# Block-sparse attention and a cosine MLP: one transfer that transposes P for two units, and query halves copied by VectorE

## The chip, the cores and the metric

The kernel runs on one core of a Trainium2 chip. The metric is the device time of one execution in microseconds. Work is spread over TensorE (PE, matrix products), VectorE (DVE), ScalarE (ACT), GpSimd (POOL) and SyncE (SP). SP computes nothing here: it issues every transfer of the kernel, in order, on one queue (SPq in the rows), and 16 DMA engines move the data.

## What is computed

Four batches, 8 heads, 768 positions, 64 columns per head, blocks of 32 positions (24 blocks). Attention is masked by blocks, and its output, 3072 x 512, goes through a feed-forward part of width 2048:

```python
scores = scale * np.matmul(q, k.transpose(0, 1, 3, 2))
mask = np.abs(blk_i - blk_j) <= 1
mask = mask | (blk_i == 0) | (blk_j == 0) | (blk_i == n_blocks - 1) | (blk_j == n_blocks - 1)
for qb in range(n_blocks):
    for kb in sampled_blocks[qb]:
        mask[qb*block:(qb+1)*block, kb*block:(kb+1)*block] = True
scores = np.where(mask, scores, -1000000000.0)
attn = np.exp(scores - np.max(scores, axis=-1, keepdims=True))
attn = attn / (np.sum(attn, axis=-1, keepdims=True) + 1e-09)
attn_out = np.matmul(attn, v)
x = attn_out.transpose(0, 2, 1, 3).reshape(B * S, H * D)
h = x @ w_in
out = (h * np.cos(h)) @ w_out
```

The weights are float64, the rest float32; the result is float32. The kernel works in float16 pairs: each number is split into a high and a low half, and a product is the sum of three products of halves.

## The kernel before, in words

The 3072 query rows are 24 blocks of 128 rows, n = 0 to 23, six per batch. The first five of a batch (n % 6 < 5) are sparse: each 32-row query block sees 8 key blocks (3 drawn, 3 of the window, 2 ends). The sixth is dense: the 3 x 32 rows at the end of the sequence and the 32 at its start see most or all keys. A sparse block has four units j = 0 to 3 of two heads each; a dense block has eight units, one head each, in two parts of 384 keys.

One unit runs like this (`attend`, from line 568, and the methods of `Steps` that it calls):

- `qk` (line 1344 sparse, 1355 dense): TensorE, scores from U (the transposed query, two orders of its halves) and W (the transposed keys) into PSUM tile sp.
- `mx` (1370) and `nb` (1384 to 1387): VectorE adds the mask and takes the row maximum, then its negative, scaled.
- `ex` (1392): ScalarE, exp into tile P with a row sum.
- `ph` (1409): ScalarE writes the high half of P into a slot of `ring`. `pl` (1413): VectorE writes the low half beside it.
- `PT` (1432): SP issues a DMA transpose of the slot into a slot of `PT`. For n = 2 alone TensorE and ScalarE transpose instead (`p_flip`, `p_put`; PARAMS PTE).
- `pv` (1443 sparse, 1458 dense): TensorE, values from PT and V (gathered by 14 to 16 transfers for a sparse block and 2 for a dense one, lines 1290 to 1306) into PSUM tile xp.

After the units of a block, `rs`, `rr`, `no`, `xh`, `xl` (1471 to 1484) normalize and split, and `xT` (1487) transposes the block into xT. Two blocks make one tile m of the feed-forward part: `m` (TensorE, 1624), cosine (ScalarE, 1641) times the input (VectorE, 1647), split into g (1709, 1712), `d` (TensorE, 1721), scaled out (1733 to 1740), stored (1745).

A block's query is loaded (1221), split (`qhi` 1081, `qlo` 1084) and transposed by `uT` (1254) into `U[:, 0]`. Its two 64-row halves are exchanged into `U[:, 1]` by `uc`, two transfers (1259 and 1261). For n = 0 to 3 TensorE makes both orders instead (`u_flip`, `u_put`; PARAMS UPE).

At the start, while the first blocks are attended, the float64 weights are turned to float32 bits (1530 to 1534), scaled and split (1084 and others), mostly on VectorE. At each batch's end the next batch's K and V are loaded, split (1081, 1084), and transposed (`kT`, 1167, half of the heads at a time: 512 columns) or stored for the gathers.

The order is written out by hand: `plan_kernel` creates 3397 operations with an engine, a cost and the parts of tiles they read and write, and the list POS gives each its place in one order for all engines, by number of creation. Each engine and the SP queue take their operations strictly in that order. Tiles come from pools with a fixed number of slots (`Sizes.slots`: ring 4, PT 4, P 5, sp 2, xp 2, ph 2, po 2); an operation that needs a slot waits until the earlier owner's last reader is done. PARAMS and the costs give positions only where POS has none.

```python
for x, (Pt, R, PT) in enumerate(zip(Pts, Rs, PTs)):
    op("ACT", ..., lambda Pt=Pt, R=R: e.p_hi(n, Pt.t, R.t), r=[Pt], w=[(R, 0)], name=f"ph{n}_{j}{tail}")
    op("DVE", ..., lambda Pt=Pt, R=R: e.p_lo(n, Pt.t, R.t), r=[Pt, (R, 0)], w=[(R, 1)], name=f"pl{n}_{j}{tail}")
    op("SP", 0, ..., lambda R=R, PT=PT: e.p_transpose(n, R.t, PT.t), r=[R], w=[PT], name=f"PT{n}_{j}{tail}")
```

Of the kernel before, what the change touches and what calls it, by code (L numbers as in the profile page):

```python
# [12 lines left out]
F16 = mybir.dt.float16  # L13
# [7 lines left out]
P = 128  # L21
# [15 lines left out]
SPR = 9  # L37
# [287 lines left out]
def plan_kernel(env, B, H, S, D, DM, DFF, pr, general=False):  # L325

    pl = Plan(() if general else POS)
    e = env
# [554 lines left out]
class Steps(Sizes):  # L883
# [523 lines left out]
    def p_hi(self, n, Pt, R):  # L1407
        p, hi, _ = self.halves(n, Pt, R)
        self.nc.scalar.copy(hi, p)  # L1409
# [398 lines left out]
```

## Time and profile before

| | us |
|---|---|
| median of 3 runs | 809.89 (806.74 to 816.49) |
| the profiled execution, its own time | 811.79 |
| its span, first to last instruction | 809.9 |
| matmuls busy (PE) | 690.1 |
| ScalarE busy | 598.7 |
| VectorE busy | 549.5 |
[...]

The rows come from that one profiled execution; what is added up from them is compared with 811.79, and the median lies 1.9 below it. Matmuls are pipelined, so a busy TensorE is not TensorE at its peak. A wait names what came last before the engine went on; the profile shows issues on SP with their own duration, apart from the time until the data have landed.

### The profile page before, as it was taken

How to read it: one execution, taken by the hardware profiler on the slowest of the kernel's cores; microseconds unless marked ns; L12 is line 12 of the kernel's file. 1: busy time of each engine (PE TensorE's matmuls, PEld its weight loads, DVE VectorE, ACT ScalarE, POOL GpSimd, SP SyncE). 2: the span in 40 equal slices, each digit the busy share in tenths (PEclk: the TensorE clock that was granted, in tenths of full speed). 3: DMA queues.
4: the chain of work that ended last, by engine and by line, in shares of the span. 5: the costliest groups of instructions: out<-in, count | busy, mean ns of one | idle time of the engine just before them, and what ended most of it. 6: DMA issues, size and time to landing. Idle time of an engine off the chain costs nothing.

```text
span 809.9 us, 27174 instructions
## 1 busy us (share of the span) xinstructions
PE 690.1 (85%) x10953; PEld 480.0 (59%) x10953; DVE 549.5 (68%) x1606; ACT 598.7 (74%) x1216; POOL 18.6 (2%) x42
## 2 busy tenths in 40 slices
PE   3355559899997789898799899997989999999995
PEld 2244446676575547575567647755667567667662
DVE  4999989998767766677486575766775745655222
ACT  2677878899669867877689698978887857867131
POOL 3500000000000000000000000000000000000000
PEclk9655669999999899999899999999999999999998
DMA  8889999999999999999998998998989977864010
GB/s 318 257 258 228 212 223 218 221 203 234 223 188 183 190 188 199 194 188 190 168 175 174 193 194 218 193 183 172 154 166 200 162 160 142 187 114 74 14 40 31
DMA packets 249015, 146.40 MB, mean 181 GB/s; under 512 B 206256, under 2 KB 206384, under 8 KB 248880
## 3 DMA queue, kind: packets, MB, share of 16 engines
q1 hardware_dynamic: 248880, 144.57, 88.7%
q8 instruction: 88, 1.44, 0.8%
q14 instruction: 47, 0.39, 0.2%
HBM read 77.67 MB, written 12.58 MB: 111 GB/s over the span
## 4 chain that ended last, share of the span: by engine, by line
PE 43%; DVE 17%; DMA 16%; ACT 11%; issue 6%; SPq 5%; DVEq 1%; ACTq 0%
PE ph L1624 18%; PE po L1721 17%; DMA PT<-ring 5%; DMA W<-kn 3%; PE sp L1344 3%; DVE P L1370 2%; ACT P L1392 2%; PE xp L1443 2%; ACT junk L1067 2%; DVE ring L1413 2%; DMA stage<-in_k_dram 2%; DMA V<-scr 2%; SPq L1432 2%; DMA xT<-n 2%; DMA U<-U 1%
## 5 line engine op out<-in xcount | busy, mean ns | idle before, releaser
L1624 PE MATMUL ph<-xT,w 128*128 128x256 f16 x2304 | 274.5, 277 | 9.5 <-DVE hs L1647 3.8
L1721 PE MATMUL po<-w,g 128*128 128x512 f16 x1152 | 264.5, 380 | 4.8 <-issue 3.8
L1624 PEld LDWEIGHTS <-w 128*128 128x128 f16 x2304 | 226.3, 99 | 49.8 <-issue 9.4
L1721 PEld LDWEIGHTS <-g 128*128 128x128 f16 x1152 | 109.8, 98 | 128.6 <-issue 6.7
L1392 ACT ACTIVATE P<-P,sm 128x256 f32<-128x256 f32 (+1 forms) x224 | 139.3, 622 | 22.9 <-DVE sm L1387 17.8
L1413 DVE TENSOR_TENSOR ring<-P,ring 128x512 f16<-128x512 f32 (+1 forms) x144 | 89.9, 627 | 59.5 <-ACT ring L1409 57.3
L1641 ACT ACTIVATE g<-ph,sm 128x512 f32<-128x512 f32 x96 | 72.4, 772 | 45.5 <-PE ph L1624 45.0
L1647 DVE SCALAR_TENSOR_TENSOR hs<-ph,sm,g 128x512 f32<-128x512 f32 x80 | 58.7, 748 | 55.2 <-ACT g L1641 54.7
L1409 ACT CAST ring<-P 128x512 f16<-128x512 f32 (+1 forms) x144 | 80.2, 565 | 17.2 <-DMA PT<-ring 15.0
L1344 PE MATMUL sp<-W,U 128*32 128x64 f16 (+1 forms) x2560 | 60.9, 248 | 19.7 <-DVE sm L1370 4.8
L1370 DVE CUSTOM_DVE_ANT_1 P<-sp,bias 128x256 f32<-128x256 f32 x160 | 61.9, 419 | 23.1 <-PE sp L1344 22.4
L1712 DVE TENSOR_TENSOR g<-hs,g 128x1024 f16<-128x1024 f32 x48 | 58.3, 1220 | 17.4 <-ACT g L1709 17.2
L1344 PEld LDWEIGHTS <-U 128*32 128x32 f16 x2560 | 47.7, 109 | 31.6 <-issue 20.9
L1709 ACT ACTIVATE g<-hs 128x1024 f16<-128x1024 f32 x48 | 50.1, 1050 | 14.5 <-DVE hs L1647 14.4
L1443 PE MATMUL xp<-V,PT 128*32 128x64 f16 x3840 | 44.4, 201 | 16.7 <-DMA PT<-ring 8.7
L1443 PEld LDWEIGHTS <-PT 128*32 128x32 f16 x3840 | 38.3, 98 | 28.3 <-issue 16.5
L1370 DVE CUSTOM_DVE_ANT_1 P<-sp,dbias 128x384 f32<-128x384 f32 x64 | 35.2, 553 | 10.3 <-PE sp L1355 6.7
L1392 ACT ACTIVATION_READ_ACCUMULATOR P<-P,sm 128x1 f32 x224 | 41.9, 187 | 0.0
L1641 ACT ACT_TABLE_LOAD x30 | 38.5, 1283 | 0.5
L1173 ACT COPY W<-W 128x256 f16 (+1 forms) x112 | 33.7, 376 | 6.8 <-DMA W<-kn 6.8
L1392 ACT ACT_TABLE_LOAD x29 | 37.2, 1283 | 1.7 <-DVE sm L1385 1.2
L1355 PE MATMUL sp<-W,U 128*128 128x384 f16 x128 | 30.0, 326 | 4.6 <-DVE sm L1370 4.5
(153 smaller groups left out, 636.5 us busy)
## 6 DMA issues: line engine op xcount, KB each, us to landing
V<-scr SPq DMA_DIRECT2D x240, 64.0 KB, 3.4
V<-scr SPq DMA_DIRECT2D x40, 384.0 KB, 5.9
stage<-in_k_dram SPq DMA_DIRECT2D x12, 512.0 KB, 4.7
w<-in_moe_w_in_dram SPq DMA_DIRECT2D x12, 512.0 KB, 6.3
w<-in_moe_w_out_dram SPq DMA_DIRECT2D x12, 512.0 KB, 4.9
V<-scr SPq DMA_DIRECT2D x8, 768.0 KB, 5.5
scr<-n SPq DMA_DIRECT2D x21, 256.0 KB, 3.9
qs<-in_q_dram SPq DMA_DIRECT2D x20, 256.0 KB, 4.5
```

Of the source, the lines that this page charges most:

```text
L1344: mm(o, U[:, z, h, rows], k, start=(a == 0 and z == 0 and part == 0), stop=(a == 1 and z == 1 and part == 1), tile_position=(0, BLK * j),)
L1370: self.nc.vector.tensor_tensor_reduce(out=self.head_cols(n, a, Pt).rearrange("p (n c) -> p n c", c=BLK), in0=self.head_cols(n, a, sp).rear ...
L1392: self.nc.scalar.activation(Pv, Pv, AF.Exp, scale=qc[:, 4:5], bias=nb[:, bcol : bcol + 1], accum_out=sums[:, 2 * j + a : 2 * j + a + 1],)
L1409: self.nc.scalar.copy(hi, p)
L1413: self.nc.vector.tensor_tensor(lo, p, hi, ALU.subtract)
L1443: mm(xp[32 * j : 32 * j + 32, h, :], PT[:, 4 * a + 2 * l + c, 32 * j : 32 * j + 32], V[:, j, c, h, d0:d1], start=(a == 0 and c == 0 and x ...
L1624: self.nc.tensor.matmul(ph[:, ff, :], self.W1[p][:, wl, cc, c * P : (c + 1) * P], xT[:, xl * NCC + cc, :], start=(j == 0), stop=(j == len( ...
L1641: self.nc.scalar.activation(self.half_cols(g, h), ph.rearrange("p f t -> p (f t)"), AF.Sin, scale=self.turns[b][:, p : p + 1], bias=self.h ...
L1647: self.nc.vector.scalar_tensor_tensor(self.half_cols(hs, h), ph.rearrange("p f t -> p (f t)"), c, self.half_cols(g, h), op0=ALU.mult, op1= ...
L1709: self.nc.scalar.activation(g[:, 0:1024], hs, AF.Copy)
L1712: self.nc.vector.tensor_tensor(g[:, 1024:2048], hs, g[:, 0:1024], ALU.subtract)
L1721: self.nc.tensor.matmul(po, g[:, gl, ff, t * P : (t + 1) * P], self.W2[p][:, wl, ff, :], start=(first and ff == half * hf and j == 0), sto ...
```

## The change

Four things change together. First, one DMA transpose covers two units: the units j and j + 1 of a sparse block, or both 384-key parts of a dense unit. Slots of ring and PT are twice as large, and there are two of each instead of four. `PT` is created after the second unit's low half, and both units' values read the one tile; for n = 2 TensorE still transposes each unit by itself. Second, `uc` becomes two copies on VectorE within SBUF. Third, the constant SPR becomes a list with the same value for each block, and costs that the planner assumes change (they move nothing, as POS has all places). Fourth, POS is a new list, for 3327 operations: 70 transposes fewer, and 40 operations moved from SP to VectorE. TensorE keeps 704 operations, ScalarE 776; VectorE goes from 1189 to 1229, SP from 723 to 613. Read off the lists: exp and cosine take turns on ScalarE 60 times in either; between a query's `qlo` and the first of its copies stand at least 13 VectorE operations; ahead of `xl` of n = 1 stand 232 VectorE operations, in the old list 225.

```diff
-SPR = 9
+SPR = [9, 9, 9, 9, 9]
...
 POS = [
-    1, 3, 15, 7, 8, 23, 31, 2, 32, 4, 102, 12, 13, 16, 17, 18, 27, 35, 38, 39, 40, 41, 42, 103, 59, 44, 192, 58, 29, 91, 1065, 46, 990, 1225, 1047,
...
 ]
...
         for k in range(0 if by_pe else 2):
-            op("SP", 0, pos, lambda k=k: e.u_swap(U.t, k), r=[(U, 0)], w=[(U, 1 + k)], dma=0.364, hw=0.625, name=f"uc{n}")
+            op("DVE", 0.36, pos, lambda k=k: e.u_swap(U.t, k), r=[(U, 0)], w=[(U, 1 + k)], name=f"uc{n}_{k}")
...
-            sps, Pts, Rs, PTs = ([Val(c) for _ in parts] for c in ("sp", "P", "ring", "PT"))
+            sps, Pts = ([Val(c) for _ in parts] for c in ("sp", "P"))
+            if not sparse or j % 2 == 0:
+                R, PT = Val("ring"), Val("PT")
+            y0 = j % 2 if sparse else 0
...
-            for x, (Pt, R, PT) in enumerate(zip(Pts, Rs, PTs)):
+            for x, Pt in enumerate(Pts):
+                y = x + y0
...
-                else:
-                    op("SP", 0, pos + at(5) + pr["PTD"] + 0.01 * x, lambda R=R, PT=PT: e.p_transpose(n, R.t, PT.t), r=[R], w=[PT], dma=1.16 if sparse else 0.87, hw=0.63, name=f"PT{n}_{j}{tail}")
-            if sparse:
-                op("PE", 0.38, vpos, lambda j=j, PT=PTs[0], xp=xp: e.sparse_values(2 * j, PT.t, V.t, xp.t),
-                   r=[PTs[0], V], w=[(xp, 2 * j), (xp, 2 * j + 1)], name=f"pv{n}_{j}", mode=(1, 1))
+                elif y:
+                    op("SP", 0, pos + at(5) + pr["PTD"] + 0.01 * x, lambda R=R, PT=PT: e.p_transpose(n, R.t, PT.t), r=[(R, (z, l)) for z in range(2) for l in range(2)], w=[(PT, 0), (PT, 1)], dma=2.32 if sparse else 1.74, hw=0.63, name=f"PT{n}_{j}{tail}")
+            for z in ((j - 1, j) if j % 2 else ()) if sparse else ():
+                op("PE", 0.38, vpos, lambda z=z, PT=PT, xp=xp: e.sparse_values(2 * z, PT.t[:, 8 * (z % 2) : 8 * (z % 2) + 8], V.t, xp.t),
+                   r=[(PT, z % 2), V], w=[(xp, 2 * z), (xp, 2 * z + 1)], name=f"pv{n}_{z}", mode=(1, 1))
...
-        qs=[None], U=[None] * 2, P=[None] * 5, ring=[None] * 4, PT=[None] * 4,
+        qs=[None], U=[None] * 2, P=[None] * 5, ring=[None] * 2, PT=[None] * 2,
...
-        s["ring"] = slots("ring", n["ring"], [P, 1024], F16)
-        s["PT"] = slots("PT", n["PT"], [P, 8, P], F16)
+        s["ring"] = slots("ring", n["ring"], [P, 2048], F16)
+        s["PT"] = slots("PT", n["PT"], [P, 16, P], F16)
...
     def u_swap(self, U, k):
         D = self.D
         if k:
-            self.nc.sync.dma_start(U[D : 2 * D, 1], U[0:D, 0])
+            self.nc.vector.tensor_copy(U[D : 2 * D, 1], U[0:D, 0])
         else:
-            self.nc.sync.dma_start(U[0:D, 1], U[D : 2 * D, 0])
+            self.nc.vector.tensor_copy(U[0:D, 1], U[D : 2 * D, 0])
...
     def p_transpose(self, n, R, PT):
-        k = self.chunks(n)
+        k = 2 * self.chunks(n)
         self.nc.sync.dma_start_transpose(PT[:, :k], R[:, : k * P])
```

The other methods (`halves`, `p_hi`, `p_lo`, `p_flip`, `p_put`, `dense_values`) only take the half of the slot that a unit owns.

## Rows read from the trace of the kernel before

**Rows 1.** The page, busy time of each engine over the span.

```profile
PE 690.1 (85%) x10953; PEld 480.0 (59%) x10953; DVE 549.5 (68%) x1606; ACT 598.7 (74%) x1216; POOL 18.6 (2%) x42
```

**Rows 2.** Busy time in stretches: length, engines, granted clock, DMA share, GB/s.

```profile
core 0: us, PE busy (x) PEld busy (x) DVE busy (x) ACT busy (x) POOL busy (x), PEclk, DMA share, GB/s
30.00:210.00 180.00, 127.53 (x2373) 92.00 (x2374) 168.66 (x446) 150.89 (x319) 2.98 (x3) 0.79 1.04 228
210.00:690.00 480.00, 437.68 (x7393) 302.59 (x7392) 314.02 (x1006) 377.88 (x790) 0.00 (x0) 0.97 0.98 182
240.00:300.00 60.00, 47.22 (x1033) 30.89 (x1032) 40.91 (x155) 46.96 (x112) 0.00 (x0) 0.91 1.02 190
390.00:420.00 30.00, 25.43 (x366) 16.46 (x364) 17.13 (x66) 22.15 (x54) 0.00 (x0) 0.89 1.08 168
...
780.00:810.00 30.00, 21.32 (x129) 12.10 (x127) 5.06 (x16) 3.88 (x5) 0.00 (x0) 0.89 0.07 21
```

**Rows 3.** TensorE's waits, 210 to 690 us: total, times, longest (us).

```profile
PE xp L1443 <- DMA PT<-ring: 7.7, 5, 2.5
PE xp L1458 <- DMA PT<-ring: 6.3, 5, 2.0
...
PE xp L1443 <- DMA V<-scr: 3.3, 2, 1.8
...
PE sp L1344 <- DMA U<-U: 2.0, 1, 2.0
...
PE xp L1458 <- DMA V<-scr: 1.1, 1, 1.1
...
PE ph L1624 <- DMA xT<-n: 0.2, 1, 0.2
```

**Rows 4.** Issues on SP by line: duration ns min/median/max, first and last start.

```profile
L1432 SPq DMA_TRANSPOSE PT<-ring x140: 1209/1260/3974, 62.0 to 743.8; - x140
...
L1167 SPq DMA_TRANSPOSE W<-kn x36: 1188/1216/2462, 216.2 to 568.2; - x36
...
L1259 SPq DMA_DIRECT2D U<-U x20: 467/584/1417, 89.9 to 650.9; - x20
```

**Rows 5.** The timeline of SP, 252 to 259 us: start, duration (us).

```profile
252.57 1.23 SPq L1432 DMA_TRANSPOSE PT<-ring  x1
253.90 4.05 SPq L1254 DMA_TRANSPOSE U<-n  x1
258.13 0.44 SPq L1306 DMA_DIRECT2D V<-scr  x1
```

**Rows 6.** Slots of ring and PT: landings, waits, lines, dense values 160 to 250.

```profile
PT<-ring SPq DMA_TRANSPOSE x140, 3.6
...
W<-kn SPq DMA_TRANSPOSE x38, 3.2
...
ACT ring L1409 <- DMA PT<-ring: 11.7, 9, 2.3
...
SPq L1432 <- PE xp L1443: 13.9, 9, 4.2
...
L1413 DVE TENSOR_TENSOR ring<-P,ring 128x384 f16<-128x384 f32 x64 | 35.3, 554 | 23.7 <-ACT ring L1409 23.6
...
L1409 ACT CAST ring<-P 128x384 f16<-128x384 f32 x64 | 31.7, 506 | 13.4 <-DMA PT<-ring 12.6
...
L1458 PE MATMUL xp<-V,PT x144: 192/193/203, 179.2 to 213.8; 128*128 128x64 f16 x144
```

**Rows 7.** VectorE's copies by form: busy us, mean ns of one, idle before.

```profile
L1173 DVE COPY W<-W 128x256 f16 x116 | 17.1, 220 | 0.0
...
L1173 DVE COPY U<-ph 128x1024 f16<-128x1024 f16 x6 | 4.0, 681 | 0.0
```

**Rows 8.** The chain that ended last, 60 to 130 us: start, duration (us).

```profile
96.00 6.78 DMA U<-U
...
116.05 7.10 PE ph L1624 x48
```

More of the change, by code (lines that the diff above doesn't have):

```diff
@@ L385, in load_regs @@
         x = pr["XD"][i]
-        eng, cost, p = (("DVE", 0.05 + 0.236 * XE[i], pr["RG"][i]), ("ACT", 0.05 + 0.236 * (12 - XE[i]), pr["RA"][i]), ("DVE", 0.05 + 0.236 * (x - XE[i]), 200.0 + i), ("SP", 0.05 + 0.236 * SPR, -200.0 + i), ("SP", 0.05 + 0.236 * (12 - SPR), pos))[which]
+        eng, cost, p = (("DVE", 0.05 + 0.236 * XE[i], pr["RG"][i]), ("ACT", 0.05 + 0.236 * (12 - XE[i]), pr["RA"][i]), ("DVE", 0.05 + 0.236 * (x - XE[i]), 200.0 + i), ("SP", 0.5 + 0.22 * SPR[i], -200.0 + i), ("SP", 0.5 + 0.22 * (12 - SPR[i]), pos))[which]
         op(eng, cost, p, lambda: e.load_regs(i, which), r=[sxv], w=[regs[i, which]], name=f"regs{i}_{which}", after=after)
@@ L541, in gather_v @@
                 x = 3 * j + s
-                if x == SPR:
+                if x == SPR[i]:
                     load_regs(i, 4, [by["ksc0s"], *[o for o in pl.ops[-400:] if o.name.startswith(f"vi{n - 1 - (n % 6 == 0)}_3_")]], ipos + 0.8)
-                op("SP", 0, ipos + 0.8 + j * 0.5, lambda j=j, s=s: e.v_drawn(n, V.t, j, s), r=[scr[b], regs[i, 3 + (x >= SPR)]], w=[(V, ("d", j, s))], dma=0.35, hw=0.5, name=f"vi{n}_{j}_{s}")
+                op("SP", 0, ipos + 0.8 + j * 0.5, lambda j=j, s=s: e.v_drawn(n, V.t, j, s), r=[scr[b], regs[i, 3 + (x >= SPR[i])]], w=[(V, ("d", j, s))], dma=0.35, hw=0.5, name=f"vi{n}_{j}_{s}")
     def gather_k(n, pos):
@@ L602, in attend @@
                    r=[nb, u], w=[(Pt, a), (sums, (j, a))], table="exp", name=f"ex{n}_{j}_{a}")
-            for x, (Pt, R, PT) in enumerate(zip(Pts, Rs, PTs)):
+            for x, Pt in enumerate(Pts):
+                y = x + y0
                 tail = "" if sparse else f"_{x}"
-                op("ACT", 0.54 if sparse else 0.45, pos + at(3) + pr["PH"] + 0.01 * x, lambda Pt=Pt, R=R: e.p_hi(n, Pt.t, R.t), r=[Pt], w=[(R, 0)], name=f"ph{n}_{j}{tail}")
-                op("DVE", 0.6 if sparse else 0.47, pos + at(4) + pr["PL"] + 0.01 * x, lambda Pt=Pt, R=R: e.p_lo(n, Pt.t, R.t), r=[Pt, (R, 0)], w=[(R, 1)], name=f"pl{n}_{j}{tail}")
+                op("ACT", 0.54 if sparse else 0.45, pos + at(3) + pr["PH"] + 0.01 * x, lambda Pt=Pt, R=R, y=y: e.p_hi(n, Pt.t, R.t, y), r=[Pt], w=[(R, (y, 0))], name=f"ph{n}_{j}{tail}")
+                op("DVE", 0.6 if sparse else 0.47, pos + at(4) + pr["PL"] + 0.01 * x, lambda Pt=Pt, R=R, y=y: e.p_lo(n, Pt.t, R.t, y), r=[Pt, (R, (y, 0))], w=[(R, (y, 1))], name=f"pl{n}_{j}{tail}")
                 flip = pr["PTE"][n] if n < 6 else 0
@@ L610, in attend @@
                     on_act = flip == 1
-                    op("PE", 0.83 if sparse else 0.63, pos + at(5) + pr["PTD"], lambda R=R, tp=tp: e.p_flip(n, R.t, tp.t), r=[R, ident], w=[tp], name=f"PT{n}_{j}{tail}")
-                    op("ACT" if on_act else "DVE", 0.904 if on_act else 0.598, pos + at(5) + pr["PTD"], lambda tp=tp, PT=PT, on_act=on_act: e.p_put(n, tp.t, PT.t, on_act), r=[tp], w=[PT], name=f"pp{n}_{j}{tail}")
-                else:
-                    op("SP", 0, pos + at(5) + pr["PTD"] + 0.01 * x, lambda R=R, PT=PT: e.p_transpose(n, R.t, PT.t), r=[R], w=[PT], dma=1.16 if sparse else 0.87, hw=0.63, name=f"PT{n}_{j}{tail}")
-            if sparse:
-                op("PE", 0.38, vpos, lambda j=j, PT=PTs[0], xp=xp: e.sparse_values(2 * j, PT.t, V.t, xp.t),
-                   r=[PTs[0], V], w=[(xp, 2 * j), (xp, 2 * j + 1)], name=f"pv{n}_{j}", mode=(1, 1))
-            else:
-                op("PE", 0.525, vpos, lambda j=j, PTs=PTs, xp=xp: e.dense_values(j, PTs, V.t, xp.t), r=[*PTs, V], w=[(xp, j)], name=f"pv{n}_{j}")
+                    op("PE", 0.83 if sparse else 0.63, pos + at(5) + pr["PTD"], lambda R=R, tp=tp, y=y: e.p_flip(n, R.t, tp.t, y), r=[(R, (y, 0)), (R, (y, 1)), ident], w=[tp], name=f"PT{n}_{j}{tail}")
+                    op("ACT" if on_act else "DVE", 0.904 if on_act else 0.598, pos + at(5) + pr["PTD"], lambda tp=tp, PT=PT, on_act=on_act, y=y: e.p_put(n, tp.t, PT.t, on_act, y), r=[tp], w=[(PT, y)], name=f"pp{n}_{j}{tail}")
+                elif y:
[3 more added lines that the diff above has]
+                   r=[(PT, z % 2), V], w=[(xp, 2 * z), (xp, 2 * z + 1)], name=f"pv{n}_{z}", mode=(1, 1))
+            if not sparse:
+                op("PE", 0.525, vpos, lambda j=j, PT=PT, xp=xp: e.dense_values(j, PT.t, V.t, xp.t), r=[(PT, 0), (PT, 1), V], w=[(xp, j)], name=f"pv{n}_{j}")
         rs, y = Val("rs"), Val("ot")
@@ L1009, in load_regs @@
         self.regs[i, which] = self.nc.values_load_multi_w_load_instructions(
-            self.sx[0:1, x + (0, XE[i], XE[i], 0, SPR)[which] : x + (XE[i], 12, d, SPR, 12)[which]],
+            self.sx[0:1, x + (0, XE[i], XE[i], 0, SPR[i])[which] : x + (XE[i], 12, d, SPR[i], 12)[which]],
             engines=[(ENG.DVE, ENG.Activation, ENG.DVE, ENG.SP, ENG.SP)[which]],
@@ L1304, in v_drawn @@
         x = 3 * j + s
-        reg = self.regs[i, 3][x] if x < SPR else self.regs[i, 4][x - SPR]
+        reg = self.regs[i, 3][x] if x < SPR[i] else self.regs[i, 4][x - SPR[i]]
         self.nc.sync.dma_start(to, self.scr[b][bass.ds(reg, BLK), :])
@@ L1399, in exp, with halves, p_hi, p_lo @@
         )
-    def halves(self, n, Pt, R):
+    def halves(self, n, Pt, R, y):
         w = self.width(n)
         k = 2 if self.seq[n][1] < self.NS else 1
-        R = R[:, : 2 * k * w].rearrange("p (a l c) -> p a l c", a=k, l=2)
+        R = R[:, 2 * k * w * y : 2 * k * w * (y + 1)].rearrange("p (a l c) -> p a l c", a=k, l=2)
         return Pt[:, : k * w].rearrange("p (a c) -> p a c", a=k), R[:, :, 0], R[:, :, 1]
-    def p_hi(self, n, Pt, R):
-        p, hi, _ = self.halves(n, Pt, R)
+    def p_hi(self, n, Pt, R, y):
+        p, hi, _ = self.halves(n, Pt, R, y)
         self.nc.scalar.copy(hi, p)
-    def p_lo(self, n, Pt, R):
-        p, hi, lo = self.halves(n, Pt, R)
+    def p_lo(self, n, Pt, R, y):
+        p, hi, lo = self.halves(n, Pt, R, y)
         self.nc.vector.tensor_tensor(lo, p, hi, ALU.subtract)
@@ L1416, in chunks, with p_flip, p_put @@
         return 8 if self.seq[n][1] < self.NS else 6
-    def p_flip(self, n, R, tp):
-        tp = self.flat16(tp)
-        for k in range(self.chunks(n)):
-            self.nc.tensor.transpose(out=tp[:, k], in_=R[:, k * P : k * P + P], identity=self.ident)
-    def p_put(self, n, tp, PT, on_act):
+    def p_flip(self, n, R, tp, y):
+        tp, c = self.flat16(tp), self.chunks(n)
+        for k in range(c):
+            x = (c * y + k) * P
+            self.nc.tensor.transpose(out=tp[:, k], in_=R[:, x : x + P], identity=self.ident)
+    def p_put(self, n, tp, PT, on_act, y):
         k = self.chunks(n)
-        self.copy(PT[:, :k], self.flat16(tp)[:, :k], on_act)
+        self.copy(PT[:, k * y : k * y + k], self.flat16(tp)[:, :k], on_act)
     def x_put(self, tp, xT, r, on_act):
@@ L1450, in sparse_values, with dense_values @@
                         )
-    def dense_values(self, h, PTs, V, xp):
+    def dense_values(self, h, PT, V, xp):
         D, NT = self.D, self.NT
@@ L1459, in dense_values @@
                     xp[:, h, :],
-                    PTs[t // 3].t[:, 3 * l + t % 3, :],
+                    PT[:, 6 * (t // 3) + 3 * l + t % 3, :],
                     V[:, t, h, d0:d1],
```

264 rows, old and new, of the table POS are left out of this document.

## The prediction

> **What bounds the kernel now.** Start with the busy shares [rows 1]: TensorE has 690.1 us of matmuls in a span of 809.9 us, ScalarE 598.7, VectorE 549.5. An average hides stages, so the next view is the busy time by stretch [rows 2]. From 30 to 210 us VectorE is busy 168.7 of 180 us and TensorE 127.5: weights are split there, and VectorE sets the pace. From 210 to 690 us TensorE is busy 437.7 of 480 and VectorE only 314.0; TensorE sets the pace, with 42.3 us of holes. In the last 30 us it lacks another 8.7, the tail behind the last matmul. The holes gather where a batch ends and the next begins: 12.8 us lie in 240 to 300, 4.6 in 390 to 420, and there the granted clock falls as well (0.91 and 0.89 against 0.97 over the whole stretch). So whatever shortens the kernel must close holes between 210 and 690, or take work off VectorE before 210.
>
> The view of waits says what ends the holes [rows 3]: the 17 rows of TensorE there sum to 41.6 us. Transfers end 20.4 of them: transposed P 7.7 + 6.3, gathered V 3.3 + 1.1, exchanged query halves 2.0. They all go out on one in-order queue, SP's, and that queue is nearly full when the holes come: a transpose occupies it for 1.26 us in the median, and the timeline shows issue behind issue without room, a transpose of the query holding it for 4.05 us [rows 4, 5]. A late P is here mostly a late issue.
>
> **The change part by part.** *Merged transposes.* There are 140 on the chip now (the block on TensorE's path, n = 2, is not among them, and is not merged later either), so 70 go. What one of twice the size costs on SP no row shows. The nearest rows are two sizes [rows 4]: K's halves, 512 columns, take 1.216 us; P, 768 or 1024 columns, 1.260. Doubling hardly shows; the bounds are 1.26 (no growth) and 2.52 (all growth). I take an estimate of 1.3, near the first. So 70 x 1.26 = 88 us leave SP less about 3.
>
> [...]
>
> *Exchanged halves.* 40 issues of about 0.58 us go from SP, 23 us [rows 4]; 40 copies of 64x1024 f16 come to VectorE. The rows are a copy of 256 columns in SBUF, 0.220 us, and of 1024 from PSUM, 0.681 [rows 7]; 40 copies are between 9 and 27 us, and I take an estimate of 0.38 each, 15 us, nearer the SBUF row since source and type agree. VectorE has 166 us idle between 210 and 690, which hides most; of 15 us I charge 2. The copies wait for the query's transpose, and VectorE is in order, so everything behind a late one waits. In the new list each stands 13 or more VectorE operations behind the split that feeds that transpose, so I price this wait at nothing; were half the 40 late by 1 us, it would be 20 us on VectorE.
>
> *Before 210 us.* The chain there passes through an exchange that took 6.78 us [rows 8]. That wait goes, but VectorE is busy 168.7 of 180 us around it, so what is late next is VectorE itself. Four copies (n = 4 and 5) are added there, 1.5 us, and the new list puts 232 operations ahead of the end of the second block's normalization where the old one has 225. Gain and loss: nothing, within 5 us either way.
>
> *Longer hold of buffers.* Four single slots for P's split halves and its transpose become two double ones. The first unit of a pair now waits for the second, and a slot comes free when a double transfer has landed. Landing takes 3.2 us for the small and 3.6 for the larger transpose [rows 6]; doubled I take an estimate of 4.4 (the same step of 0.4 again for each 512 columns), with bounds 3.6 and 7.2. A dense head holds a slot 0.51 + 0.51 + 0.55 + 4.4 = 6.0 us, so two slots allow a head every 3.0 us (before: (0.51 + 0.55 + 3.6) x 2 / 4 = 2.3). The densest stretch has eight heads from 179.2 to 213.8 us, one in 5.0 [rows 6]. It fits, with less slack. ScalarE already waits here 9 times, 11.7 us, and SP waits 9 times, 13.9 us, for a transposed tile to be read. Each of ScalarE's nine may grow by half of the 0.8 us: I charge 3.5 us, bounds 0 and 42 (the slower rival).
>
> *The order anew.* Nearly every position changes. The alternations between exp and sin on ScalarE stay 60, and the products are the same, so the new list brings no work of its own; I take 0, within 10 us either way.
>
> **The sum.** 111 us of SP's issue time go. Of the 20.4 us that transfers cost TensorE I take four fifths back, 16.3: what is left is landing, which no shorter queue removes. The lower clock: (1 - 0.97) x 437.7 = 13.1 us of TensorE's busy time, of which transfers own 20.4/41.6; times four fifths, 5.1. Against it 2 for the copies and 3.5 for the holds. Together -16.3 - 5.1 + 2 + 3.5 = -15.9. The profiled execution took 811.8, which becomes 795.9; the median of the runs, 809.9, lies 1.9 lower, so the forecast is 794.
>
> **The rivals.** *The queue hid more.* ScalarE's and VectorE's own waits start with late transfers too, and nearly all holes close: (41.6 + 13.1) x 0.8 = 43.8 less, 5.5 more, 772. For it: SP without room just where the holes are [rows 5]. Against it: half of the waited time names an engine or issue, not a transfer.
>
> *Issue time goes with size.* Then 70 x 2.52 replaces 140 x 1.26, and only the exchange's 23 of 111 us leave SP: -21.4 x 23/111 + 5.5 = +1.1 on 811.8, and 811 by the median. For it: transposes that held SP up to 4 us [rows 5]; against it the two sizes of rows 4.
>
> *Two slots are too few (the other side).* Place: ScalarE's high half of P, which needs a free slot, and everything queued behind it, exp and cosine. With 1.6 us to fill and 1.5 us for a transposed tile to be read (13.9/9), a slot held longer than 2 x 5.0 us stalls every dense head; that is decided by a landing beyond 6.9 us, and twice 3.6 is 7.2. Price: 32 heads by 1.3 us (11.7/9) is 42 us, so 811.8 + 42 - 21.4 + 2 - 1.9 = 832. For it: it happens already with four slots. Against it: the step from 3.2 to 3.6 us.
>
> **How the numbers follow.** Forecast 0.50, split evenly by the bound of 2% (793.7 us; about what a measurement of this kernel can tell from no change) as its centre lies on it. Queue hid more: 0.17, all faster. Issue with size: 0.15, nearly all within 2%, 0.01 slower. Slots: 0.18, 0.15 slower and 0.03 within. So faster 0.42, within 2% 0.42, slower 0.16. The forecast's own range is 784 to 806 (order and start, 10 us either way). Reaching into the outer cases until about two tenths are left, 774 to 824.
>
> **What would show it.** Right: 70 transposes of P at 1.3 to 1.5 us on SP; no exchange on SP and 40 copies near 0.38 us on VectorE; TensorE's waits for P, V and U between 210 and 690 well below 20 us; its clock there above 0.97; about the same time up to 210. Wrong: merged issues above 2 us, landings of 7 us with ScalarE's wait for ring slots above 30 us, VectorE waiting on the query's transpose, or a first multiplication of the feed-forward that starts more than 5 us from 116 us [rows 8].

## The result, and the profile after

| | before | after |
|---|---|---|
| median (4 runs each, same chip) | 810.17 us (806.74 to 816.49) | 789.74 us (788.36 to 790.37) |
| ratio, 95% interval | | 0.9737 (0.9675 to 0.9798) |
| the profiled execution | 811.79 us | 788.36 us |
| its span, mean granted TensorE clock (share of full speed) | 809.9 us, 0.928 | 786.6 us, 0.941 |

The kernel is 2.6% faster, and 794 was forecast. Lines shift by a few: P's transpose is now line 1434, the exchange 1260 and 1262, scores 1345 and 1356, values 1445 and 1460, the high half 1410 and the low half 1414.

The page's busy line after, to be read beside [rows 1]:

```profile
PE 678.8 (86%) x10953; PEld 473.1 (60%) x10953; DVE 565.0 (72%) x1646; ACT 597.9 (76%) x1216; POOL 17.1 (2%) x42
```

TensorE does the same 10953 matmuls in 11.3 us less busy time, and the span shrinks by 23.3; so 12.0 us of holes are gone. The 11.3 are put down to the clock: busy time times mean granted clock, summed over 0 to 30, 30 to 210, 210 to 690 and the rest, is 646 us in both (646.4 and 646.3). Where the gain lies, the stretches tell (columns as in [rows 2]):

```profile
0.00:30.00 30.00, 10.61 (x143) 8.95 (x143) 20.69 (x59) 11.74 (x18) 17.06 (x42) 1.00 0.90 313
30.00:210.00 180.00, 124.15 (x2350) 91.53 (x2350) 165.39 (x433) 149.06 (x315) 0.00 (x0) 0.75 0.97 219
210.00:690.00 480.00, 455.84 (x7692) 315.76 (x7693) 343.97 (x1081) 397.23 (x826) 0.00 (x0) 1.00 0.95 182
```

Nothing is gained before 210 us: from 30 to 210 TensorE is busy 3.4 us less than before, with 23 matmuls fewer. The whole gain lies from 210 to 690, where it is busy 455.8 us in place of 437.7, at a clock of 1.00 in place of 0.97. Its waits there after, beside [rows 3]:

```profile
PE xp L1445 <- DMA V<-scr: 3.4, 4, 2.2
PE xp L1460 <- DMA PT<-ring: 3.0, 4, 1.3
...
PE xp L1460 <- DMA V<-scr: 1.7, 1, 1.7
...
PE sp L1345 <- DVE U L1260: 0.9, 1, 0.9
...
PE ph L1626 <- DMA xT<-n: 0.7, 1, 0.7
...
PE sp L1345 <- DVE U L1262: 0.5, 1, 0.5
```

The rows of this view sum to 23.1 us where there were 41.6. Transfers end 8.8 of them (3.4 + 3.0 + 1.7 + 0.7), and the values of sparse blocks have no wait for P left in this stretch (7.7 before).

So far all goes as forecast. The rows of the two edits don't. First the tile PT: the duration of an issue on SP in ns (min/median/max), ScalarE's wait for a slot from 210 to 690 us (total, times, longest), and the landing in us (min/median/max):

```profile
L1434 SPq DMA_TRANSPOSE PT<-ring x70: 1316/2253/7578, 64.9 to 719.5; - x70
...
ACT ring L1410 <- DMA PT<-ring: 11.6, 10, 2.4
...
DMA to landing us min/median/max: 3.7/5.1/11.0
```

There are 70 transposes in place of 140, but one holds SP for 2.25 us in the median where 1.3 was assumed. Added up issue by issue over the trace, P's transposes took 210.0 us on SP before and 187.8 now, and all issues together 560.3 and 516.3. So 44 us left SP, not 111: 22 with P, 26 with the exchange, and the other issues grew by 4. The timeline shows the range of a merged issue (start, duration in us):

```profile
137.81 7.58 SPq L1434 DMA_TRANSPOSE PT<-ring  x1
...
673.92 1.93 SPq L1434 DMA_TRANSPOSE PT<-ring  x1
...
677.06 1.32 SPq L1434 DMA_TRANSPOSE PT<-ring  x1
...
700.70 1.43 SPq L1434 DMA_TRANSPOSE PT<-ring  x1
```

Of the 70 merged issues 16 are below 1.5 us (1.32 to 1.48), of the 140 single ones before, 103. How long SP had issued nothing does not decide it: the one at 677.06 follows another issue by 0.2 us and takes 1.32, the one at 673.92 comes after 5.1 us without an issue and takes 1.93.

Second the exchange, tile U (forms, then what ended VectorE's waits):

```profile
L1260 DVE COPY U<-U x20: 420/421/423, 77.6 to 629.5; 64x1024 f16<-64x1024 f16 x20
L1262 DVE COPY U<-U x20: 422/423/424, 99.4 to 628.2; 64x1024 f16<-64x1024 f16 x20
...
  DVE U L1262: 4.2, 3
  DVE U L1260: 3.2, 3
```

40 copies by 0.42 us are 17 us on VectorE, and it waits 7.4 us for the query's transposes in front of them.

If merging saved only a quarter of what was assumed and the time fell all the same, something else paid. That is what the experiments are about.

### The profile page after: what moved, and what is told of

Read it like the earlier page. It is cut to its first block, busy times and chain, and to the rows that moved or that the text cites. A ratio compares the mean times of both kernels' runs of the same rounds, so it can differ in the third digit from the quotient of the medians.

```text
span 786.6 us, 26927 instructions
## 1 busy us (share of the span) xinstructions
PE 678.8 (86%) x10953; PEld 473.1 (60%) x10953; DVE 565.0 (72%) x1646; ACT 597.9 (76%) x1216; POOL 17.1 (2%) x42
## 4 chain that ended last, share of the span: by engine, by line
PE 40%; DVE 18%; DMA 17%; ACT 12%; issue 6%; SPq 6%; DVEq 1%; ACTq 0%
PE ph L1626 17%; PE po L1723 16%; DMA PT<-ring 5%; ACT P L1393 3%; DMA W<-kn 3%; DMA V<-scr 3%; DVE P L1371 3%; DVE ring L1414 2%; PE sp L1345 2%; SPq L1307 2%; DMA w<-in_moe_w_out_dram 2%; PE xp L1445 2%; ACT ring L1410 2%; DMA w<-in_moe_w_in_dram 1%; DMA U<-n 1%
## 5 line engine op out<-in xcount | busy, mean ns | idle before, releaser
L1626 PE MATMUL ph<-xT,w 128*128 128x256 f16 x2304 | 270.1, 275 | 4.7 <-DMA xT<-n 2.7
L1626 PEld LDWEIGHTS <-w 128*128 128x128 f16 x2304 | 224.0, 99 | 44.2 <-DMA xT<-n 3.7
L1414 DVE TENSOR_TENSOR ring<-P,ring 128x512 f16<-128x512 f32 (+1 forms) x144 | 87.8, 625 | 37.7 <-ACT ring L1410 36.7
L1410 ACT CAST ring<-P 128x512 f16<-128x512 f32 (+1 forms) x144 | 78.2, 566 | 15.5 <-DMA PT<-ring 13.7
L1345 PE MATMUL sp<-W,U 128*32 128x192 f16 (+1 forms) x2560 | 57.9, 240 | 23.4 <-DVE sm L1371 11.1
L1345 PEld LDWEIGHTS <-U 128*32 128x32 f16 x2560 | 45.8, 106 | 38.6 <-issue 29.8
L1445 PE MATMUL xp<-V,PT 128*32 128x64 f16 x3840 | 41.5, 201 | 14.5 <-DMA PT<-ring 6.2
L1445 PEld LDWEIGHTS <-PT 128*32 128x32 f16 x3840 | 36.9, 97 | 24.2 <-issue 14.6
```

The lines of the kernel that those rows point to most:

```text
L1345: mm(o, U[:, z, h, rows], k, start=(a == 0 and z == 0 and part == 0), stop=(a == 1 and z == 1 and part == 1), tile_position=(0, BLK * j),)
L1414: self.nc.vector.tensor_tensor(lo, p, hi, ALU.subtract)
L1445: mm(xp[32 * j : 32 * j + 32, h, :], PT[:, 4 * a + 2 * l + c, 32 * j : 32 * j + 32], V[:, j, c, h, d0:d1], start=(a == 0 and c == 0 and x ...
L1626: self.nc.tensor.matmul(ph[:, ff, :], self.W1[p][:, wl, cc, c * P : (c + 1) * P], xT[:, xl * NCC + cc, :], start=(j == 0), stop=(j == len( ...
```

## Experiments

Each time is the median of its runs, each ratio is against the kernel before on the same chip. POS goes by number of creation, so each kernel has its own copy of a list; an operation that the list's own kernel doesn't have is placed as said.

### Which part pays: the exchange by itself

`copies_alone` is the kernel before, with all its 140 single transposes and its old order; only the exchange goes to VectorE, each copy half way between the exchange's old place and the block's first scores.

```diff
-            op("SP", 0, pos, lambda k=k: e.u_swap(U.t, k), r=[(U, 0)], w=[(U, 1 + k)], dma=0.364, hw=0.625, name=f"uc{n}")
+            op("DVE", 0.36, pos, lambda k=k: e.u_swap(U.t, k), r=[(U, 0)], w=[(U, 1 + k)], name=f"uc{n}_{k}")
...
-            self.nc.sync.dma_start(U[D : 2 * D, 1], U[0:D, 0])
+            self.nc.vector.tensor_copy(U[D : 2 * D, 1], U[0:D, 0])
```

> The kernel before, with its list, and only the exchange made by VectorE, half way between its old place and the first scores. Theory Q: a fifth of the gain, 4 us, so 805 us. Theory C: 800 or less. Theory L: 808 to 815, as VectorE now waits for the query's transpose at places that were not chosen for it; that wait should then show on VectorE.

Measured: 789.96 us, ratio 0.9778 (0.9716 to 0.984). That is the time of the whole change, and theory C's range. The stretch from 210 to 690 us of `copies_alone`, TensorE's waits for P in it, and the issues of P:

```profile
210.00:690.00 480.00, 449.90 (x7575) 311.94 (x7576) 343.48 (x1076) 396.55 (x823) 0.00 (x0) 1.00 0.96 182
```

```profile
PE xp L1443 <- DMA PT<-ring: 3.0, 2, 2.1
PE xp L1458 <- DMA PT<-ring: 2.5, 3, 1.2
```

```profile
L1432 SPq DMA_TRANSPOSE PT<-ring x140: 1210/1239/3416, 61.7 to 720.1; - x140
```

The waits for P fall from 14.0 [rows 3] to 5.5 us though not one transpose was merged, and the clock comes to 1.00 as well.

The reverse: `copies_queue` is the changed kernel with the exchange back on SP's queue, at the copies' places.

```diff
-            self.nc.vector.tensor_copy(U[D : 2 * D, 1], U[0:D, 0])
+            self.nc.sync.dma_start(U[D : 2 * D, 1], U[0:D, 0])
```

> The changed kernel, with the exchange of the query's halves back on SP's queue (40 transfers, at the places where the copies stand). Theory Q (a shorter queue is what gained): 23 us of issues return to SP, a fifth of what I thought went, so about 794 us (790 + 4). Theory O (the new list of places is what gained, whatever the transfers): 789 to 792. Theory C (the copies are what gained, as an exchange took several us to land before scores could start): 800 or more, with TensorE waiting over 10 us for U.

Measured: 835.32 us, ratio 1.0337 (1.028 to 1.0393), 45 us over the changed kernel. But part of this is the place: SP stands before the exchange until the query's transpose has landed. SP's waits over the span, and TensorE's from 210 to 690:

```profile
SPq L1262 <- DMA U<-n: 20.3, 6, 5.6
...
SPq L1260 <- DMA U<-n: 11.3, 5, 3.7
```

```profile
PE sp L1345 <- DMA U<-U: 22.3, 9, 5.8
```

`copies_queue_early` has the same edit, with the exchange up to 8 operations of SP behind the query's transpose, ahead of the first scores.

> The changed kernel with the exchange back on SP's queue, now issued 8 SP operations behind the query's transpose (or half way to the first scores of that block where fewer lie between), so that it can land before it is needed. If copies_queue was slow only because its exchanges stood where a copy of 0.42 us is in time and a transfer is not, this comes back to 793 to 800 us, and the copies themselves are worth little. If the copies are worth much by themselves (theory C), it stays above 812.

Measured: 813.45 us, ratio 1.0043 (1.0008 to 1.0077). That is above the 812 of theory C; whether its reason holds, that an exchange lands late, is asked below. With this the four corners stand:

| | exchange by transfer | exchange by VectorE |
|---|---|---|
| single transposes, old order | 809.7 | 790.0 |
| merged transposes, new order | 813.5 | 789.7 |

Along a row the exchange is worth 20 to 24 us. Down a column merging with its order is worth nothing. (The corner of 813.5 has its places from this study; a list made for it might do better.)

`copies_early` asks whether VectorE's place for the copies can still be bettered: `copies_alone` with each copy at 0.15 of the way in place of a half.

> copies_alone with the copies nearer to the transpose: 0.15 of the way from the exchange's old place to the first scores, instead of 0.5. In copies_alone a copy starts 9 us or more after the transpose was issued and TensorE and VectorE still stood waiting for it 16 us in all. If that wait is on the path: 780 to 787 us, faster than both kernels. If scores come in time anyway: 788 to 792. If VectorE now waits for transposes: above 792, with that wait in its list.

Measured: 794.25 us, ratio 0.9782 (0.9714 to 0.985). No better. No version beat the changed kernel and `copies_alone`, which tie.

### What it is in the exchange that costs 20 us

Taking a transfer away does three things: the chain from query to scores is shorter, SP has 40 issues fewer, and the DMA engines have 40 transfers fewer. `extra_transfers` is `copies_alone` with 40 added transfers of the same size into a spare place in DRAM, at the exchange's old places in SP's order; nothing needs their data, and in the trace one copy of VectorE waits 0.4 us for one of them. The short chain stays, the load on SP and on the DMA engines returns.

```diff
+        for k in range(0 if by_pe else 2):
+            op("SP", 0, pos, lambda k=k: e.u_extra(U.t, k), r=[(U, 0)], dma=0.364, hw=0.625, name=f"ue{n}")
...
+        self.nc.sync.dma_start(self.spare[k], U[D * k : D * k + D, 0])
```

> copies_alone, with 40 transfers of the same size put back on SP's queue at the exchange's old places; they read the transposed query and write it to memory that nobody reads, so that they load the queue and the DMA engines but nothing waits for them. Theory L2 (what gained is the chain: query transposed, exchanged, scores, and everything in order behind them): stays at 788 to 796 us. Theory Q2 (what gained is the room on the queue): back to 803 to 812.

Measured: 809.72 us, ratio 0.9985 (0.9953 to 1.0016). The gain is gone, to the microsecond. Its stretch and the added transfers:

```profile
210.00:690.00 480.00, 437.15 (x7414) 300.86 (x7413) 333.04 (x1050) 381.46 (x796) 0.00 (x0) 0.98 0.95 184
```

```profile
spare<-U SPq DMA_DIRECT2D x40, 128.0 KB, 3.0
```

That is the range of theory Q2. TensorE's busy time from 210 to 690 is that of before to 0.5 us. So the shorter chain by itself is worth nothing. On SP all issues sum to 562 us here, 560 before and 524 in `copies_alone`: of these 38 us the added transfers' own issues are 24, and P's transposes take 211 us where they take 198 without them.

`exchange_gpsimd` is the kernel before with the exchange issued by GpSimd, on a queue of its own. Chain and transfers stay, SP has 40 issues fewer.

```diff
-            self.nc.sync.dma_start(U[D : 2 * D, 1], U[0:D, 0])
+            self.nc.gpsimd.dma_start(U[D : 2 * D, 1], U[0:D, 0])
```

> The kernel before, with its list and places, but the exchange is issued on GpSimd's queue, which is idle. SP's queue is relieved as in copies_alone, the chain still holds a transfer. Theory L2: 805 to 815 us, as the exchange still lands several us after the transpose. Theory Q2: 788 to 796.

Measured: 806.44 us, ratio 0.995 (0.991 to 0.9989). That is the range of theory L2, which the run before had ruled out: neither theory holds in both. SP's issues sum to 539 us, so 21 us are freed and not the 36 of `copies_alone`, as P's transposes still take 215 us there; and only some 4 of the 20 us come. Its stretch, and the landing of the exchange, before and in this run:

```profile
210.00:690.00 480.00, 441.62 (x7467) 304.86 (x7465) 319.67 (x1021) 385.32 (x800) 16.44 (x32) 0.98 0.99 186
```

```profile
U<-U SPq DMA_DIRECT2D x40, 128.0 KB, 3.4
```

```profile
U<-U POOLq DMA_DIRECT2D x40, 128.0 KB, 4.4
```

By the interval that is 1 to 7 us, and the exchange lands 1 us later here, which may hide a part. Nor is it the same transfer on another queue in every respect: the 40 go as 1920 packets here and as 3200 on SP's queue. Still, 21 of 36 us of SP's room would be worth 12 of the 20 if room alone counted. What both slow kernels have and the fast one lacks is 40 transfers on the DMA engines, whose mean busy share in this stretch was 0.98 before [rows 2]. That these engines are the limit is not shown: the share is 0.95 with the added transfers and 0.96 in `copies_alone` without them. The 40 transfers may also cost by stretching other issues on SP, and SP's room and the chain may each hold the kernel where the other is freed. The run that would tell these apart, `copies_alone` with the added transfers on GpSimd's queue, was not made; this stays open.

### What merging is worth

`two_transfers` is the changed kernel, places and slots as they are, with each double transpose issued as two halves back to back.

```diff
-        k = 2 * self.chunks(n)
-        self.nc.sync.dma_start_transpose(PT[:, :k], R[:, : k * P])
+        k = self.chunks(n)
+        for y in range(2):
+            self.nc.sync.dma_start_transpose(PT[:, k * y : k * y + k], R[:, k * P * y : k * P * (y + 1)])
```

> The changed kernel, with each double transpose issued as two of half the size, back to back at the same place, same slots. Theory Q with a fixed issue cost: 70 issues of 1.26 us return to SP, 88 us, and the time goes up by four fifths of the gain, to about 806 us. Theory O, and a queue that is held by transfers not yet moved rather than by a fixed cost: two halves hold SP as long as one double (2 x 1.4 against 2.8 us in the mean), so 789 to 793 us, and SP's total on these issues stays within 190 to 215 us.

Measured: 799.13 us, ratio 0.9875 (0.9843 to 0.9906). The issues of P:

```profile
L1435 SPq DMA_TRANSPOSE PT<-ring x140: 1209/1274/4558, 65.8 to 730.3; - x140
```

Two halves take 2 x 1.27 us in the median where a double one takes 2.25, and all of them 227 us where merged they take 188, above the 190 to 215 of the second theory; the time lies between the two. So in the new order merging saves 39 us on these issues (27 over all issues of SP) and 9.4 us of the kernel's time. That is a real gain, but only against two transfers that both wait for the pair, as this order has it.

`no_merge` takes that wait away too: the changed kernel with single transposes in four single slots, each where its data allow. For a first unit of a pair, which has no place in the new list, that is behind its low half or shortly before the second one's.

```diff
-        k = 2 * self.chunks(n)
+        k = self.chunks(n)
...
-        qs=[None], U=[None] * 2, P=[None] * 5, ring=[None] * 2, PT=[None] * 2,
+        qs=[None], U=[None] * 2, P=[None] * 5, ring=[None] * 4, PT=[None] * 4,
```

> New list and copies on VectorE, but P transposed unit by unit into four single slots as before; the first unit's transfer stands right behind its low half where four slots allow it (43 of 70), else ahead of the second's. Theory Q: 806 us, as merging is most of the queue's relief. Theory O: 785 to 792 us, since half of P lands earlier and nothing else changes. The rival that pairs cost something by their longer hold says below 788.

Measured: 862.37 us, ratio 1.0651 (1.06 to 1.0703). SP's wait for the low half over the span, of `no_merge` and then of the changed kernel:

```profile
SPq L1432 <- DVE ring L1413: 85.2, 30, 8.0
```

```profile
SPq L1434 <- DVE ring L1414: 40.4, 12, 8.5
```

That is outside every range. A transpose that was put early makes the whole queue stand until VectorE has written the low half. This run says what a badly placed issue costs on an in-order queue, not what merging is worth.

`no_drawn` asks what stretches a merged issue. It is the changed kernel without the gathers of drawn V blocks from n = 2 on (24 of 240 remain in its rows, so 216 are gone, and the values of these blocks are made from other data).

```diff
+        if n >= 2:
+            return
```

> The changed kernel without the transfers of drawn value rows for blocks n = 2 and later (192 of 240 small gathers left out, so values of drawn blocks are stale; nothing else changes). It measures what holds SP on a double transpose. If transfers not yet moved hold it: the median issue falls from 2.25 us to 1.3 to 1.6 and the longest (7.6) below 5. If the double size itself costs it: the median stays at 2.1 to 2.3.

Measured once: 760.82 us. The issues of P and the stretch:

```profile
L1436 SPq DMA_TRANSPOSE PT<-ring x70: 1274/2019/6149, 65.0 to 691.9; - x70
```

```profile
210.00:690.00 480.00, 473.34 (x8006) 330.56 (x8003) 355.99 (x1114) 412.76 (x850) 0.00 (x0) 1.00 0.83 159
```

The median of an issue goes only from 2.25 to 2.02 us, between the two expectations. These gathers aren't what mainly stretches it; what does was not found. (The sum falls from 187.8 to 174.2 us.) The 29 us that go with the gathers' load show how much the transfers still cost the changed kernel.

### What the order is worth

`order_alone` runs the operations of before in the new list, with the single transposes placed as in `no_merge` and the exchange where the new list has the copies. No line of code but POS changes.

> The kernel before in all its operations (140 single transposes, four slots, exchange on the queue), with the new list of places (the first unit's transposes placed as in no_merge). Theory Q: no relief at all, so 805 to 812 us. Theory O: nearly all of the gain, 788 to 796 us. In between (797 to 804) the order and the transfers share it.

Measured: 894.16 us, ratio 1.1021 (1.0965 to 1.1077). That is slower than any theory said. TensorE's longest wait from 210 to 690 us is for the exchange:

```profile
PE sp L1344 <- DMA U<-U: 30.0, 8, 9.0
```

It has the faults of `copies_queue` and `no_merge` together. `order_alone_2` mends both: the two single transposes stand at the pair's place, and the exchange early.

> All operations of the kernel before with the new list, placed kindly: the two single transposes of a pair stand at one place, as in two_transfers, and the exchange as in copies_queue_early. Theory O (the list alone gained): 790 to 797 us. If merging and copies each cost what they cost in two_transfers and copies_queue_early and these add, it is the sum of the two differences over 790. Theory L (the list is only good for the operations it was made for): above 810.

Measured: 830.28 us, ratio 1.0251 (1.0187 to 1.0316). The two parts undone one at a time cost 9.4 (`two_transfers`) and 23.7 (`copies_queue_early`) over 789.7, together 823; the measured 830 has 7 us that the parts don't explain. That is theory L's range.

`structure_old_order` is the reverse, the changed kernel's operations in the old list (105 operations moved back to where their data and the slots allow).

> All operations of the changed kernel with the list of the kernel before: double transposes at the place of the pair's second, copies half way between the exchange's place and the first scores, 105 operations moved back where two double slots would not hold. Theory Q (fewer issues gain in any list): 790 to 800 us. Theory L: not faster than before, 812 to 840, as the pair's second unit was placed for a transfer of its own.

Measured: 859.33 us, ratio 1.0635 (1.0568 to 1.0703), above both ranges. TensorE's two longest waits from 210 to 690 us, and ScalarE's wait for a slot of `ring`:

```profile
PE sp L1356 <- DVE sm L1371: 14.8, 9, 3.6
PE xp L1445 <- DMA PT<-ring: 13.2, 5, 4.6
```

```profile
ACT ring L1410 <- DMA PT<-ring: 41.4, 17, 5.5
```

In the old list, with 105 places from this study, the merged transposes, with the wait for the pair and two slots, cost 69 us over `copies_alone` (859.3 - 790.0). ScalarE stands 41.4 us for a slot, where it stands 11.7 before and 2.2 in `copies_alone`, with four single slots, and 11.6 in the changed kernel: two double slots do hold ScalarE up in an order that was not made for them. The new list takes this back, and no more.

## Why the prediction was right, and where it was not

**What bounds the kernel: right.** The holes from 210 to 690 us shrank from 42.3 to 24.2 us and nothing came before. Of the 20.4 us that transfers ended there, 16.3 were to come back; with 0.5 for xT, which the prediction left out, they went from 20.9 to 8.8, so 12.1 came. The other waits, for which 5.5 was charged, fell instead, from 20.7 to 14.3 (41.6 - 20.9 and 23.1 - 8.8). Of these 18.5 us the stretch before 210 gave 6.4 back, and over the span the holes shrank by 12.0, where the sum had 10.8. The clock was the term too small: 5.1 was taken and 11.3 came, as it stood at 1.00 over the whole stretch. Together 23.3 by the profile, against 15.9; by the medians 20.4.

**Merged transposes: the step that failed.** "So 70 x 1.26 = 88 us leave SP less about 3": 22 left. The estimate of 1.3 us is what the shortest take (1.32 to 1.48 us in 16 of 70); the median is 2.25 and the mean 2.68. The median misled for the single ones as well: 140 took 210.0 us, 1.50 each in the mean. The two sizes of [rows 4] were read as evidence that size doesn't count, while the timeline of [rows 5], with a transpose that held SP for 4.05 us, warned that a median is not what an issue costs in this queue. (The 111 us of the sum are 88 + 23, without the 3 that this step took off.) The step's other bound, 2.52 for an issue that grows with size, comes nearer to the median; the 16 short issues don't agree with it.

**Exchanged halves: undervalued by far.** By the prediction they were 23 of the 111 us of SP's time, so a fifth of the 21.4 us, 4.4, less 2 for the copies. Alone they are worth 20 us in the old order and 24 in the new, the whole change. The step took every microsecond of SP's time as equal, whoever uses it. `exchange_gpsimd` shows that taking these issues off SP brings some 4 us while the transfers stay, and `extra_transfers` that the 40 transfers with their issues are what must go; why they cost so much is open. The copies' price was near: 0.42 us against 0.38. The step priced VectorE's wait for the query's transpose at nothing; it is 7.4 us, and TensorE waits 1.4 us (0.9 + 0.5) for the copies from 210 to 690.

**Before 210 us: the chain held, the work fell a little short.** The first multiplication of the feed-forward starts at 116.9 us where it was 116.05 [rows 8]. TensorE has done 134.8 us of work by 210 (10.61 + 124.15) in place of 141.1 (13.60 + 127.53). That is 6.4 us less, a little more than the 5 that were allowed, and from 30 us on at a mean clock of 0.75 in place of 0.79. The first 30 us before, beside [rows 2]:

```profile
0.00:30.00 30.00, 13.60 (x147) 11.26 (x147) 18.38 (x53) 10.98 (x17) 15.58 (x40) 0.89 0.89 295
```

**Longer hold: the size about right, the charge not seen.** A double transpose lands in 5.1 us (4.4 estimated, 3.6 to 7.2 as bounds). ScalarE's wait for slots from 210 to 690 us is 11.6 us where it was 11.7 [rows 6], so the 3.5 charged for it did not come in the new order. In the old one ScalarE waits 41.4 us.

**The order: nothing, but not on its own.** "I take 0" came out for merging and order together (the columns of the table above), not for the list: the operations of before in the new list are slower by 2.5% or more, the new ones in the old list by 6.4%.

**The rivals.** Two slots too few (832): fell for this kernel by ScalarE's row; its place and about its price (42 us) show in `structure_old_order`. Issue goes with size (811): its premise was half right and its time wrong, since the gain did not hang on merging. The queue hid more (772): the run without the gathers reached 761, so more could be had, but from load, and this change did not have it. That 794 came near is luck: two errors of opposite sign met, 22 us of SP's time in place of 85 and 20 us for the exchange in place of 2.

## What to carry to other kernels

A saving of issue time counts only for what an issue costs in that queue: look for issues of the same kind that take much longer than their median (here 3.97 us against 1.26) before crediting fewer and larger ones. When several edits land together, run each alone with an order that suits it: here an edit of three lines and 40 places had all of the gain, and the large one with its new order had none. A small transfer inside SBUF can cost more than its place in the chain or in the queue shows, 0.5 us each here; an engine that has room did it in 0.42 us. And an exchange of lists says little: operations in a list that was made for others ran 2.5 to 10% slower.

## What was not expected of the hardware

The issue of one DMA transpose of 1536 or 2048 f16 columns took from 1.32 to 7.58 us on SP in the same run, and the median hardly moved (2.25 to 2.02) when 216 other transfers were left out. Forty transfers of 128 KB that next to nothing waits for cost 20 us (`copies_alone` 790.0, `extra_transfers` 809.7), 0.5 us each, as much as the exchange that everything waited for.
